# A new issue order for a block-sparse attention and FFN kernel, with thirteen zero matmuls ahead of the first key turn

## The chip, the cores and the metric

The kernel runs on one core of a Trainium2 chip. The metric is the device time of one execution in microseconds, the median of the runs shown. A core has five engines with a queue each: TensorE (PE in the profile, its weight loads PEld), VectorE (DVE), ScalarE (ACT), GpSimd (POOL) and SyncE (SP), which here only issues transfers. Each engine takes the instructions of its queue in order and waits at the head for what the instruction needs.

## The reference

Block-sparse causal attention over 4 batches, 8 heads, 768 positions of width 64, then an FFN on the joined heads. All inputs are float32.

```python
k_rep = k.reshape(B, H, 12, 64, 64).mean(axis=3)            # one mean per block of 64 keys
gate = einsum('bhsd,bhnd->bhsn', q, k_rep)                  # causal blocks only
mask = top 3 blocks of gate, and the row's own block, and key <= query
attn = softmax(where(mask, q @ k.T / 8, -1e9))
x = (attn @ v), heads side by side                          # 3072 x 512
h = x @ w_in                                                # 512 x 2048
out = gelu_tanh(h) @ w_out                                  # 2048 x 512
```

## The kernel before

The work is cut into 16 pairs of heads, p = 0 to 15, four for each batch (b = p // 4). A pair goes through these steps; the line numbers are those of the kernel before, and in the kernel after every one is one higher, since its table of the order is one line longer.

- Loads, issued on SP's queue (L386, L392; the first k and q at L420, k on SP and q on ScalarE's queue). For batch 0 they go to free parts of large tiles, for later batches to a few buffers (`ksd`, `qsd`, `vsd`), which come free when the values have been transposed or cast.
- Turning k and q. In batch 0, TensorE turns them in halves of three tiles (`turn`, L537 for k of pairs 0 and 1, with two more columns that give the sums of the blocks, and L540), and VectorE or ScalarE copies the halves out (L355 is a copy on ScalarE, L357 on GpSimd, L359 on VectorE). Later, VectorE transposes them (`tr`, L556), sums the keys' blocks (`ks`, L613; L575 in batch 0) and spreads the sums (`ksb`, L630).
- The gate (L679): q against the block sums. VectorE finds the third largest per row with MAX8 (L711) and writes a mask (`madd`, L716); TensorE turns the mask (L748), and a copy puts it below q in `qT` (L355 or L359), so that one matmul gives the masked scores.
- Scores (`heads2`, L855 in batch 0; `heads`, L1038 later), the exponential on ScalarE (L874, L1051), the causal triangle by a select on GpSimd (L900, L1065), the products with v (L923, L1077), the division on VectorE (L941, L960), and the result's transposition (`turn_out`, L980).

When a batch's four pairs are through, its FFN follows: `s1` (L1114, matmuls with w_in; L1203 for part of the last batch), GELU on ScalarE (L1126), then the product with w_out. For batch 0 that is plain (L1314). For the others it is Strassen's scheme in seven products per pair of 128-token rows (`half`, L1364), with sums of the inputs on VectorE (L1301), and joins of the products into `osb`, also on VectorE (L1413), stored by SP (L1339, L1448, L1457). Work of the FFN of one batch is interleaved with the scores of the next: it is the filler that TensorE works on while ScalarE makes exponentials. ScalarE has to load another table when it goes from exponentials to GELU and back.

The weights w_in and w_out, 2 MB each in the types of the kernel, are loaded by GpSimd's queue in two parts each (`load_w`, L452). w_in is issued after the last v of batch 0 has come in. The first loads of batch 1 are held back on SP's queue until w_in is there (`hold`, L1559).

Zero matmuls (`warm`, L1516) work on a zeroed tile into a free PSUM bank and have no reader.

Nothing is scheduled at run time or by the compiler. The program builds some 1,900 operations with their dependences, and then issues them in the order of a table; a second table says which buffer an operation takes, in the order in which buffers are asked for, and a third which copies go to ScalarE or GpSimd instead of their first choice (mostly VectorE):

```python
engine = {n: e for e, ops in ENGINE.items() for n in ops}
picks = iter(BUFFER)
for n in ORDER:
    op = self.ops[n]
    for kind, key in op.takes:
        if key not in self.buf:
            self.buf[key] = self.kinds[kind][0][next(picks)]
    op.emit(engine.get(n, next(iter(op.engines))))
```

So `ORDER` sets the order within each engine's queue, and the semaphores follow from the dependences. The four PSUM banks (`bank`) serve turns, gates, masks, products with v and the FFN's second product; two double banks (`wide`) serve scores and the FFN's first product.

Of the kernel before, what the change touches and what calls it, by code (L numbers as in the profile page):

```python
# [21 lines left out]
    6, 0, 1, 1890, 1891, 2, 1892, 1893, 1894, 3, 9, 1895, 1896, 1897, 1898,  # L22
    62, 71, 4, 15, 1899, 1900, 1901, 195, 73, 72, 1902, 64, 12, 75, 18, 22,
    5, 63, 1903, 76, 74, 77, 23, 66, 1904, 1905, 84, 85, 68, 19, 78, 89,
    1906, 26, 1907, 82, 200, 31, 67, 194, 79, 35, 90, 32, 80, 91, 98, 86,
    83, 36, 87, 100, 93, 196, 214, 99, 101, 201, 95, 205, 94, 39, 215, 102,
    197, 1908, 103, 1909, 104, 113, 206, 109, 1910, 115, 114, 1911, 219,
    210, 120, 111, 220, 1912, 118, 121, 105, 40, 106, 1913, 27, 30, 119,
    211, 198, 1914, 1915, 107, 110, 216, 122, 249, 123, 234, 202, 44, 203,
    207, 250, 208, 212, 240, 124, 221, 43, 48, 45, 217, 235, 133, 125, 229,  # L30
    224, 1916, 49, 241, 52, 222, 135, 126, 236, 140, 245, 251, 127, 53, 230,
    268, 225, 138, 57, 56, 141, 246, 129, 1917, 231, 134, 58, 263, 232, 131,
    242, 151, 1918, 238, 130, 155, 237, 243, 157, 139, 142, 269, 254, 143,
    264, 247, 252, 255, 283, 258, 144, 284, 226, 279, 274, 1919, 270, 146,
    227, 280, 256, 1920, 1921, 265, 266, 1922, 147, 145, 271, 275, 292, 276,
    288, 297, 272, 289, 302, 298, 277, 303, 281, 149, 285, 308, 309, 299,
    286, 259, 153, 290, 317, 61, 1923, 300, 293, 260, 304, 305, 318, 169,
    326, 313, 322, 294, 328, 261, 310, 295, 323, 306, 319, 363, 314, 364,
    311, 365, 163, 329, 315, 356, 358, 170, 366, 171, 359, 360, 361, 320,
    324, 327, 367, 362, 352, 353, 354, 355, 357, 330, 408, 409, 410, 411,  # L40
    331, 412, 373, 374, 335, 375, 376, 377, 174, 403, 336, 404, 405, 406,
    388, 407, 389, 175, 178, 390, 391, 393, 394, 395, 396, 392, 418, 397,
    419, 420, 179, 421, 368, 369, 182, 370, 433, 422, 434, 398, 399, 371,
    435, 400, 372, 436, 401, 437, 383, 438, 183, 439, 186, 338, 187, 440,
    402, 441, 384, 378, 385, 386, 339, 442, 443, 387, 444, 379, 380, 445,
    446, 337, 341, 381, 428, 334, 429, 190, 346, 345, 447, 191, 631, 448,
    382, 430, 423, 451, 424, 431, 452, 342, 453, 425, 432, 426, 454, 413,
    414, 632, 455, 427, 343, 344, 415, 449, 416, 456, 417, 457, 347, 458,
    584, 635, 459, 349, 460, 585, 461, 553, 588, 462, 463, 566, 348, 590,
    464, 587, 465, 466, 470, 586, 570, 595, 471, 567, 571, 639, 472, 591,  # L50
    473, 592, 636, 593, 574, 568, 474, 450, 575, 640, 561, 475, 476, 477,
    478, 583, 479, 480, 552, 562, 576, 481, 467, 554, 644, 596, 572, 692,
    645, 557, 598, 482, 483, 650, 484, 648, 485, 569, 558, 488, 622, 489,
    490, 696, 654, 491, 597, 492, 555, 486, 594, 651, 493, 573, 614, 652,
    494, 577, 623, 601, 653, 556, 578, 559, 693, 647, 560, 615, 495, 618,
    496, 563, 497, 564, 616, 498, 602, 603, 705, 605, 646, 706, 499, 619,
    656, 658, 617, 655, 500, 624, 606, 501, 609, 502, 700, 697, 503, 657,
    711, 507, 620, 708, 709, 508, 678, 621, 565, 610, 611, 607, 504, 643,
    661, 625, 715, 679, 509, 712, 626, 662, 665, 701, 713, 957, 666, 510,
    579, 674, 604, 511, 716, 512, 958, 680, 663, 608, 682, 513, 514, 714,  # L60
    612, 515, 613, 516, 675, 717, 468, 517, 718, 683, 580, 669, 961, 518,
    719, 676, 677, 707, 726, 965, 519, 664, 670, 667, 684, 520, 681, 727,
    505, 735, 736, 671, 962, 970, 668, 972, 728, 1020, 521, 722, 522, 971,
    525, 672, 723, 730, 976, 737, 685, 673, 743, 704, 523, 526, 738, 686,
    966, 527, 1024, 974, 1021, 528, 724, 627, 744, 1025, 529, 745, 1033,
    530, 731, 531, 725, 628, 732, 1034, 739, 740, 532, 729, 1037, 981, 733,
    758, 687, 533, 534, 830, 1028, 734, 1039, 741, 535, 742, 746, 756, 536,
    977, 747, 1040, 1044, 537, 748, 538, 978, 1082, 1924, 539, 831, 832,
    979, 1041, 749, 833, 759, 760, 761, 834, 540, 1083, 973, 768, 769, 770,
    762, 1042, 1086, 524, 1043, 548, 1095, 771, 1096, 544, 545, 752, 753,  # L70
    487, 754, 755, 772, 1029, 763, 764, 765, 757, 766, 840, 1087, 841, 1099,
    842, 843, 767, 782, 1036, 783, 784, 785, 844, 786, 792, 549, 793, 969,
    794, 795, 773, 1032, 835, 796, 836, 837, 982, 838, 825, 826, 546, 1035,
    1101, 774, 541, 1090, 1144, 827, 839, 828, 984, 811, 775, 829, 1145,
    812, 985, 1157, 813, 814, 1148, 1158, 815, 1161, 845, 787, 1152, 788,
    789, 1149, 1105, 1153, 790, 1163, 846, 1045, 806, 542, 807, 808, 809,
    1102, 1164, 1410, 847, 791, 801, 802, 810, 803, 1411, 980, 804, 777,
    1165, 778, 805, 1159, 779, 780, 816, 781, 817, 818, 1103, 819, 849, 850,
    1002, 1166, 1104, 797, 820, 1156, 1418, 851, 1107, 852, 821, 853, 1048,
    854, 822, 989, 988, 855, 856, 798, 859, 823, 990, 860, 1098, 857, 861,  # L80
    862, 863, 858, 799, 1091, 997, 1003, 864, 865, 547, 866, 1419, 998,
    1414, 550, 991, 551, 992, 993, 868, 1473, 1474, 994, 869, 1004, 1010,
    1047, 1011, 870, 1094, 867, 776, 871, 999, 1012, 1006, 800, 995, 1005,
    872, 1068, 873, 1007, 874, 1169, 1069, 1064, 824, 1008, 996, 1000, 875,
    1055, 1009, 877, 1065, 1072, 878, 848, 876, 1056, 1073, 879, 1051, 1109,
    1110, 1013, 1477, 880, 1059, 1066, 1478, 1052, 885, 886, 887, 1097,
    1001, 1053, 888, 1117, 1060, 1014, 1070, 889, 1067, 1061, 1106, 890,
    891, 1118, 892, 882, 881, 895, 1423, 1481, 896, 1160, 1134, 883, 1071,
    1486, 893, 897, 1119, 894, 1126, 1074, 898, 899, 900, 1167, 901, 902,
    1135, 903, 1054, 1425, 1130, 904, 1539, 1075, 1172, 905, 1127, 906,  # L90
    1121, 1131, 1136, 1057, 1132, 1424, 1535, 1058, 907, 908, 1168, 1540,
    1426, 909, 1113, 1114, 1062, 910, 1128, 1076, 911, 913, 914, 915, 1122,
    1171, 1115, 1536, 1063, 1129, 1123, 1188, 1116, 1189, 1133, 1196, 1015,
    1120, 1487, 1137, 916, 1197, 1124, 1198, 1190, 912, 1179, 917, 921,
    1077, 1192, 1125, 922, 923, 1490, 1180, 1193, 924, 1183, 925, 926, 927,
    928, 1548, 931, 932, 1181, 1488, 1194, 1184, 1138, 1415, 1139, 1185,
    1175, 933, 934, 1191, 1195, 1235, 1199, 1176, 1177, 935, 1209, 929, 936,
    1178, 1236, 937, 1422, 1543, 938, 930, 1492, 940, 1549, 1182, 1186, 941,
    1200, 942, 1211, 1212, 1597, 1482, 943, 944, 1187, 1552, 1201, 1427,
    945, 946, 1213, 1237, 947, 1202, 1496, 1238, 1598, 1489, 939, 1601,  # L100
    1429, 949, 1214, 1554, 950, 1215, 1493, 1555, 948, 1430, 1264, 1265,
    951, 1494, 1266, 1267, 1239, 1230, 1231, 1495, 1268, 1232, 1233, 1269,
    1270, 1602, 1271, 1558, 1272, 1556, 1234, 1273, 1544, 1216, 1217, 952,
    1218, 1610, 1219, 1205, 1220, 1206, 1550, 1207, 1431, 1432, 1208, 1559,
    1611, 1254, 1551, 1434, 1614, 1210, 1255, 1256, 1257, 1240, 953, 1258,
    1241, 1547, 1242, 1243, 1245, 1246, 1616, 1247, 1244, 1248, 1259, 1260,
    1261, 1497, 1262, 1249, 1221, 1485, 1222, 1223, 1263, 1433, 1557, 1224,
    1498, 919, 1288, 1289, 1225, 1290, 1501, 1617, 1291, 1250, 1283, 1284,
    1620, 918, 1292, 1285, 1286, 1287, 1251, 1500, 1278, 1274, 1279, 1280,
    1281, 1435, 1293, 1294, 1438, 1295, 1621, 1560, 1296, 1613, 1302, 1226,  # L110
    1303, 1282, 1618, 1227, 1304, 1297, 1305, 1455, 1228, 1517, 1306, 1442,
    1619, 1437, 1518, 1307, 1275, 1298, 1252, 1308, 1309, 1312, 1313, 1519,
# [1506 lines left out]
```

## Time and profile before

| | us |
|---|---|
| median of 3 runs | 257.85 (257.77 to 258.06) |
| profiled execution | 257.31 |
| its span | 255.4 |
| TensorE busy | 246.1 (96%) |
| VectorE busy | 191.2 (75%) |
| ScalarE busy | 174.8 (68%) |
| GpSimd busy | 87.6 (34%) |
| bytes moved | 32.61 MB, mean 128 GB/s |

The span is the time from the first to the last instruction that the profiler records; the execution's own time is 1.9 us longer. An engine's busy time counts its instructions and leaves out waits. TensorE's busy time flatters it, since its matmuls are pipelined and overlap: a matmul of 384 columns has a duration of 326 ns on the page, while 54 of them in a row take 8.78 us, 163 ns each.

### The profile page before, as it was taken

Reading aid. Unit: us, or ns where it says so; the run is one execution under the profiler, and the core shown is the slowest. Engines: PE = TensorE matmul, PEld = TensorE weight load, DVE = VectorE, ACT = ScalarE, POOL = GpSimd, SP = SyncE. Lnnn points to the kernel's source line nnn. Section 1 sums busy time; section 2 is a strip of 40 time slices with the busy share of each in tenths; the row PEclk is TensorE's granted clock in tenths of the full one; section 3 lists DMA queues with packets and bytes.
Section 4 is the critical chain, followed back from the end, with each engine's and each line's share of the span. In section 5 each row is a group of like instructions: output and inputs, shape, how many; then the busy total and the mean of one; then the engine's idle time right before and its main releaser. Section 6 shows DMA issues by size and latency. Waiting matters only on the chain.

```text
span 255.4 us, 6432 instructions
## 1 busy us (share of the span) xinstructions
PE 246.1 (96%) x2485; PEld 171.8 (67%) x2485; DVE 191.2 (75%) x537; ACT 174.8 (68%) x222; POOL 87.6 (34%) x168
## 2 busy tenths in 40 slices
PE   6999999999999899899999999999999999999994
PEld 5676676655556465565678888665778887666883
DVE  2588853016887997998999888999977675777953
ACT  2469887643888899667798885566999865557300
POOL 8637753002255465212175655030155410000000
PEclk9999999999999999999999999999999999999999
DMA  8998699999999899999497896930511421020024
GB/s 162 219 205 170 98 213 135 191 172 158 158 167 151 171 192 140 216 138 183 83 163 161 156 120 124 153 108 13 131 59 39 107 74 42 3 82 0 3 82 164
DMA packets 130926, 32.61 MB, mean 128 GB/s; under 512 B 124528, under 2 KB 126928, under 8 KB 130896
## 3 DMA queue, kind: packets, MB, share of 16 engines
q1 hardware_dynamic: 126160, 27.62, 61.9%
q0 software_dynamic: 3136, 4.19, 10.2%
q10 hardware_dynamic: 1600, 0.39, 0.7%
q8 instruction: 19, 0.31, 0.5%
q14 instruction: 11, 0.09, 0.1%
HBM read 27.26 MB, written 6.29 MB: 131 GB/s over the span
## 4 chain that ended last, share of the span: by engine, by line
PE 81%; DVE 6%; DMA 3%; POOL 3%; ACT 2%; SPq 1%; issue 1%; DVEq 0%; POOLq 0%; ACTq 0%
PE wide L1114 26%; PE bank L1364 22%; PE wide L1038 8%; PE wide L1203 5%; PE bank L1077 5%; PE bank L1314 4%; DMA sd<-in_k_dram 3%; PE wide L855 3%; PE bank L679 2%; PE bank L923 2%; DVE s L556 2%; SPq L392 1%; DVE ks L613 1%; PE bank L980 1%; PE bank L540 1%
## 5 line engine op out<-in xcount | busy, mean ns | idle before, releaser
L1114 PE MATMUL wide<-xT,w_in 128*128 128x384 f16 x416 | 73.8, 326 | 0.0
L1051 ACT ACTIVATE ats<-wide 128x896 f16<-128x896 f32 x72 | 62.6, 916 | 7.1 <-PE wide L1038 3.7
L1126 ACT ACTIVATE G<-wide 128x768 f16<-128x768 f32 x52 | 42.0, 810 | 27.5 <-PE wide L1114 25.4
L1114 PEld LDWEIGHTS <-w_in 128*128 128x128 f16 x416 | 39.8, 98 | 26.1 <-issue 0.8
L1065 POOL TENSOR_SCALAR_AFFINE_SELECT ats<-ats 128x256 f16<-128x256 f16 x72 | 32.4, 462 | 56.4 <-ACT ats L1051 55.9
L1038 PE MATMUL wide<-qT,kT 76*128 76x512 f16 (+3 forms) x192 | 38.9, 305 | 0.1
L556 DVE STREAM_TRANSPOSE s<-sd 128x768 f32<-128x768 f32 x24 | 23.1, 968 | 16.9 <-DMA sd<-in_k_dram 15.0
L1364 PE MATMUL bank<-w_out,G 128*128 128x256 f16 x216 | 33.4, 272 | 0.0
L1314 PE MATMUL bank<-w_out,G 128*128 128x512 f16 x96 | 29.7, 379 | 1.2 <-ACT qT L355 1.2
L1364 PEld LDWEIGHTS <-G 128*128 128x128 f16 x288 | 26.8, 98 | 5.4
L357 POOL CAST kT<-s 64x768 f16<-64x768 f32 x22 | 18.7, 854 | 29.5 <-DVE s L556 28.8
L1077 PEld LDWEIGHTS <-ats 128*128 128x128 f16 x504 | 23.0, 97 | 5.0 <-POOL v L357 0.3
L1077 PE MATMUL bank<-v,ats 128*128 128x65 f16 x504 | 25.5, 194 | 0.0
L1413 DVE TENSOR_TENSOR osb<-bank,osb 128x512 f32<-128x512 f32 (+1 forms) x38 | 22.0, 592 | 3.2 <-PE bank L1364 2.9
L1038 PEld LDWEIGHTS <-kT 76*128 76x128 f16 x192 | 17.1, 98 | 9.4 <-issue 0.6
L874 ACT ACTIVATE ats<-wide 128x1024 f16<-128x1024 f32 (+3 forms) x24 | 21.0, 919 | 3.3 <-PE wide L855 3.1
L1364 PEld LDWEIGHTS <-XS 128*128 128x128 f16 x216 | 20.1, 97 | 4.2
L1364 PE MATMUL bank<-TS,XS 128*128 128x256 f16 x144 | 22.4, 272 | 0.0
L357 POOL CAST v<-vsd 128x768 f16<-128x768 f32 x13 | 11.7, 908 | 19.0 <-DMA vsd<-in_v_dram 18.9
L961 DVE TENSOR_TENSOR xn<-bank,zr 128x384 f16<-128x384 f32 x24 | 13.4, 557 | 0.8
L1314 PEld LDWEIGHTS <-G 128*128 128x128 f16 x96 | 8.9, 97 | 7.5 <-issue 2.5
L711 DVE MAX8 sel<-sel 128x8 f32<-128x12 f32 x160 | 13.3, 157 | 0.6
(119 smaller groups left out, 360.9 us busy)
## 6 DMA issues: line engine op xcount, KB each, us to landing
out_dram<-osb SPq DMA_DIRECT2D x23, 256.0 KB
vsd<-in_v_dram SPq DMA_DIRECT2D x26, 192.0 KB
sd<-in_k_dram SPq DMA_DIRECT2D x48, 96.0 KB
sd<-in_q_dram SPq DMA_DIRECT2D x48, 96.0 KB
w_in<-in_moe_w_in_dram POOLq DMA_DIRECT2D x2, 1024.0 KB, 10.8
w_out<-in_moe_w_out_dram POOLq DMA_DIRECT2D x2, 1024.0 KB, 12.8
G<-in_k_dram SPq DMA_DIRECT2D x4, 192.0 KB
G<-in_q_dram SPq DMA_DIRECT2D x4, 192.0 KB
```

The costliest lines, as they stand in the source:

```text
L357: nc.gpsimd.tensor_copy(out=out, in_=in_)
L556: nc.vector.transpose(out=T[key + "T32", p], in_=T[key, p].rearrange("p t j -> p (t j)"))
L874: nc.scalar.activation(out=T["at", u][:, :, 0:n], in_=plan.buf[("st",) + u].rearrange("p (h w) -> p h w", h=2)[:, :, 0:n], func=AF.Exp, bi ...
L1038: nc.tensor.matmul(st[:, x:e], kT16[i][h][0:76, s0:s0 + 128], qT16[i][h][0:76, s0 + (x - cb):s0 + (e - cb)], start=True, stop=True)
L1051: nc.scalar.activation(out=T["at", u][:, 0:n], in_=plan.buf[("st",) + u][:, 0:n], func=AF.Exp, bias=0.0, scale=SCALE)
L1065: nc.gpsimd.affine_select(out=dg, in_=dg, compare_op=ALU.is_ge, fill=0.0, base=0, pattern=[[0, 2], [1, 128]], channel_multiplier=-1)
L1077: nc.tensor.matmul(pvv[:, qc, 0:65], at[:, cb + (qc - jc) * 128: cb + (qc - jc + 1) * 128], v16[i][:, jc, h, :], start=(gi == 0 and jc == ...
L1114: nc.tensor.matmul(hps[:, 512 * e:512 * e + HALF], w_in16[:, ci, (2 * j + e) * 128: (2 * j + e + 1) * 128], T["xT", b][:, ci, HALF * h:HAL ...
L1126: nc.scalar.activation(out=G[:, :, h, j, :], in_=plan.buf["hps", b, j, h].rearrange("p (e w) -> p e w", e=2)[:, :, 0:HALF], func=AF.Gelu_a ...
L1314: nc.tensor.matmul(plan.buf["ops", b, ti], G[:, f % 2, 2 * ti // NC, f // 2, ti % (NC // 2) * 128:ti % (NC // 2) * 128 + 128], w_out16[:, ...
L1364: nc.tensor.matmul(dst[:, HD * h:HD * h + HD], FACT[m][0][:, j, t * 128:(t + 1) * 128], FACT[m][1][:, j, :], start=(clear and j == 0), sto ...
L1413: nc.vector.tensor_tensor(out=dst(), in0=src(), in1=other(), op=ALU.add)
```

## The change

Only the three tables change: `ORDER`, `BUFFER` and `ENGINE`. The operations are the same, but for one zero matmul fewer (38 for 39). Of `ORDER`, which has 1,668 numbers before and 1,667 after, here are the first rows, the rows with the issue of w_out (operation 163), and the last:

```diff
 ORDER = [
-    6, 0, 1, 1890, 1891, 2, 1892, 1893, 1894, 3, 9, 1895, 1896, 1897, 1898,
-    62, 71, 4, 15, 1899, 1900, 1901, 195, 73, 72, 1902, 64, 12, 75, 18, 22,
-    5, 63, 1903, 76, 74, 77, 23, 66, 1904, 1905, 84, 85, 68, 19, 78, 89,
-    1906, 26, 1907, 82, 200, 31, 67, 194, 79, 35, 90, 32, 80, 91, 98, 86,
...
-    242, 151, 1918, 238, 130, 155, 237, 243, 157, 139, 142, 269, 254, 143,
...
-    311, 365, 163, 329, 315, 356, 358, 170, 366, 171, 359, 360, 361, 320,
...
+    4, 2, 0, 1890, 1891, 1892, 1893, 1894, 1895, 1896, 6, 1897, 15, 1898, 9,
+    1899, 1900, 1901, 12, 1, 1902, 62, 18, 71, 64, 195, 1903, 73, 72, 63,
+    75, 82, 1904, 22, 1905, 1906, 23, 76, 66, 1907, 31, 19, 74, 35, 77, 36,
+    84, 98, 68, 85, 3, 99, 5, 83, 78, 194, 44, 200, 79, 80, 100, 89, 67,
...
+    129, 126, 127, 241, 138, 231, 245, 242, 254, 139, 153, 255, 157, 1918,
+    131, 246, 140, 232, 268, 269, 238, 237, 141, 270, 142, 130, 163, 258,
...
+    1841, 1868, 1864, 1867, 1847, 1865, 1866, 1869, 1870, 1872, 1871, 1880,
+    1878, 1877, 1874, 1873, 1879, 1876, 1883, 1881, 1884, 1886, 1885, 1843,
+    1882, 1887, 1888, 1844, 1842, 1846, 1927, 1848]
...
 ENGINE = {
     "ACT": [
-        67, 72, 74, 85, 90, 110, 114, 119, 121, 139, 141, 331, 348, 449,
-        467, 486, 504, 523, 541, 580, 594, 597, 628, 657, 716, 749, 857,
-        893, 980, 981, 1043, 1044, 1105, 1167, 1168, 1202, 1496, 1620, 1621,
-        1655, 1674, 1677, 1698, 1704, 1707, 1727, 1736, 1786, 1822],
+        67, 72, 74, 90, 99, 101, 110, 114, 119, 121, 139, 331, 345, 346,
+        348, 449, 467, 486, 504, 523, 541, 580, 598, 628, 654, 657, 716,
+        749, 857, 893, 929, 980, 981, 1043, 1044, 1105, 1106, 1167, 1168,
+        1202, 1346, 1497, 1558, 1620, 1668, 1674, 1677, 1698, 1707, 1727,
+        1736, 1786, 1822],
     "POOL": [
...
-        1159, 1160, 1425, 1426, 1488, 1489, 1550, 1551, 1613]}
+        337, 586, 587, 646, 647, 707, 708, 972, 973, 1035, 1036, 1097, 1159,
+        1160, 1425, 1426, 1488, 1489, 1551, 1613]}
```

Numbers from 1890 on are the zeros; 6 and 12 are the first loads of k, 9 and 15 of q; 0 to 5 are constants; 62 and 66 turn pair 0's k, 71 and 73 its q; 75 and 78 are its gates, 194 and 200 its first scores; 89 and 93 turn pair 1's k; 157 and 163 issue w_in and w_out; 1842 to 1844 are in the seventh product of a pair of token rows of batch 3, 1846 its join and 1848 its store. In words, by engine:

- TensorE: thirteen zeros stand ahead of the first turn of keys (62), nine before. The first scores (194) stand right behind pair 0's second gate (78); the turns of pair 1's keys (89, 93), the first of which lay between, come later. Scores of pairs 4 to 7 stand closer together, with fewer of batch 0's FFN matmuls between them. The kernel's last matmuls (1844, 1842) belong to product seven of the second pair of token rows in batch 3; before they belonged to product two of the third pair.
- SP: v of pair 0 is loaded as two consecutive halves; k and q of pair 6 and the first part of k of pair 7 go ahead of v of pair 5; batch 0's results are stored later among the loads; k of pair 11 comes before that of pair 10.
- ScalarE's queue: the second half of pair 0's q is issued ahead of its first.
- GpSimd: two memsets of constants (ones) come first; w_out (163) is issued one select behind w_in (157), where ten operations lay between before.
- Engines of copies: eight go from ScalarE to VectorE, twelve the other way, two casts from GpSimd to VectorE.

More of the change, by code (lines that the diff above doesn't have):

```diff
@@ L21 @@
 ORDER = [
[128 rows of a table removed]
-BUFFER = [
[23 rows of a table removed]
[128 rows of a table added]
+BUFFER = [
[23 rows of a table added]
 ENGINE = {
     "ACT": [
[4 rows of a table removed]
[5 rows of a table added]
     "POOL": [
-        337, 586, 587, 646, 647, 707, 708, 972, 973, 1035, 1036, 1097, 1098,
-        1159, 1160, 1425, 1426, 1488, 1489, 1550, 1551, 1613]}
+        337, 586, 587, 646, 647, 707, 708, 972, 973, 1035, 1036, 1097, 1159,
+        1160, 1425, 1426, 1488, 1489, 1551, 1613]}
 class Op:
```

287 rows, old and new, of tables (BUFFER, ORDER) are left out of this document.

## The prediction

> **What bounds the kernel now.** I read the page first, then the windows by stage, then TensorE's waits, the chain of waits, and last the timelines around each place where TensorE stood still. The page of the kernel before:
>
> ```profile
> span 255.4 us, 6432 instructions
> PE 246.1 (96%) x2485; PEld 171.8 (67%) x2485; DVE 191.2 (75%) x537; ACT 174.8 (68%) x222; POOL 87.6 (34%) x168
> L556 DVE STREAM_TRANSPOSE s<-sd 128x768 f32<-128x768 f32 x24 | 23.1, 968 | 16.9 <-DMA sd<-in_k_dram 15.0
> ```
>
> TensorE is busy for 96% of the span, so a new order can gain only where TensorE stands still or goes slowly. The windows (us, then busy us of PE, PEld, DVE, ACT, POOL, then clock, DMA share, GB/s) say where:
>
> ```profile
> 0.00:10.00 10.00, 7.54 (x42) 5.59 (x43) 2.94 (x28) 2.44 (x4) 8.69 (x31) 1.00 1.01 183
> 10.00:20.00 10.00, 8.98 (x118) 6.96 (x119) 8.34 (x38) 6.59 (x12) 3.90 (x10) 1.00 1.20 213
> 60.00:80.00 20.00, 19.89 (x162) 10.46 (x160) 15.98 (x58) 15.61 (x21) 7.44 (x12) 1.00 1.03 156
> 80.00:90.00 10.00, 8.83 (x99) 5.35 (x98) 8.64 (x27) 8.14 (x11) 5.59 (x11) 1.00 0.92 178
> 90.00:100.00 10.00, 10.00 (x128) 6.51 (x127) 7.93 (x16) 9.28 (x13) 5.98 (x13) 1.00 1.15 153
> 100.00:110.00 10.00, 8.99 (x80) 5.18 (x78) 9.59 (x38) 7.42 (x10) 4.55 (x6) 1.00 1.29 186
> 110.00:180.00 70.00, 70.00 (x669) 49.24 (x667) 64.57 (x169) 51.22 (x66) 24.64 (x40) 1.00 0.77 128
> 180.00:252.00 72.00, 71.98 (x702) 55.81 (x699) 53.99 (x110) 44.89 (x54) 12.17 (x25) 1.00 0.20 62
> ```
>
> From 110 to 252 us TensorE is busy for 141.98 of 142 us: nothing is to be had there. Missing are 2.46 us before 10, 1.02 from 10 to 20, 1.17 in 80 to 90 and 1.01 in 100 to 110. The start holds more than that, because busy matmuls there overlap work that waits: its pace is set by the exponentials on ScalarE. Here are TensorE's and ScalarE's timelines (start, us, line, shape, count, idle before and its releaser):
>
> ```profile
> 1.07 2.10 PE L1516 MATMUL bank<-XS 128*128 128x256 f16 x9 [1.07 <-DVE bmask L284]
> 4.18 1.64 PE L537 MATMUL bank<-identk,G 128*128 128x130 f32 x6 [1.01 <-DMA G<-in_k_dram]
> ...
> 8.44 0.96 PE L537 MATMUL bank<-identk,G 128*128 128x130 f32 x6
> ...
> 10.22 0.37 PE L679 MATMUL bank<-s,ksbx 128*32 128x96 f32 x8
> 10.52 0.94 PE L537 MATMUL bank<-identk,G 128*128 128x130 f32 x6
> ...
> 11.61 0.28 PE L855 MATMUL wide<-XS,XS 64*128 64x256 f16 x2
> ...
> 10.32 0.37 ACT L355 COPY XS<-bank 128x256 f16<-128x256 f16 x1 [2.07 <-DVE XS L359]
> ...
> 12.35 1.51 ACT L874 ACTIVATE ats<-wide 128x1024 f16<-128x1024 f32 x2 [0.38 <-PE wide L855]
> 14.52 1.94 ACT L874 ACTIVATE ats<-wide 128x1024 f16<-128x1024 f32 x2 [0.66 <-PE wide L855]
> 18.09 0.48 ACT L355 CAST XS<-bank 128x384 f16<-128x384 f32 x1 [1.64 <-DVE ks L575]
> ...
> 38.61 1.30 ACT L874 ACTIVATE ats<-wide 128x256 f16<-128x256 f32 x2 [0.52 <-PE wide L855]
> ```
>
> The first score is at 11.61, the first exponential at 12.35, the last ends at 39.91, and the FFN of batch 0 can't begin in earnest before. Two stalls remain; the chain of waits gives both (start, us, what):
>
> ```profile
> 77.35 4.16 DMA sd<-in_k_dram
> 81.59 0.99 DVE s L556
> 82.60 0.95 DVE ks L613
> 83.59 0.50 DVE qT L359
> 84.11 0.69 ACT qT L355
> 84.84 0.59 PE bank L1314 x2
> ...
> 93.83 4.68 DMA sd<-in_k_dram
> 98.63 0.99 DVE s L556
> ...
> 101.85 0.98 DVE s L556
> 102.87 0.48 PE bank L679 x8
> ```
>
> In the first, k of pair 7 lands late, VectorE stands before its transpose (L556), and the mask copies of pair 6 (qT, on VectorE and ScalarE), which need nothing of pair 7, are queued behind it. In the second, k and q of pair 9 are late themselves, and pair 9's gate (L679) waits. TensorE's idle times there are those missing in the windows, 1.17 and 1.01. Both go back to the loads, and the loads to the weights:
>
> ```profile
> 26.72 1.66 POOL L452 DMA_DIRECT2D w_in<-in_moe_w_in_dram  x2
> ...
> 38.52 1.78 POOL L452 DMA_DIRECT2D w_out<-in_moe_w_out_dram  x2
> ...
> 41.11 9.76 SPq L392 DMA_DIRECT2D sd<-in_k_dram  x4
> ...
> 63.44 1.25 SPq L386 DMA_DIRECT2D vsd<-in_v_dram  x2
> ...
> 70.65 0.82 POOL L357 CAST v<-vsd 128x768 f16<-128x768 f32 x1
> ```
>
> The four issues of pair 4's k need 9.76 us on SP's queue, from 41.11, while w_out moves. Just ahead of that the transfers run thin, at 73 GB/s, because w_in is in and w_out was issued late:
>
> ```profile
> 40.00:42.00 2.00, 2.00 (x26) 1.35 (x23) 0.00 (x0) 1.94 (x3) 0.30 (x1) 1.00 0.83 73
> ```
>
> **The change, part by part.** Instructions keep their shapes; what changes is their order on each queue, buffers, and the engine of some twenty copies. By the two engine tables ScalarE gets four operations more, VectorE two fewer, GpSimd two fewer.
>
> Zeros. Thirteen instead of nine stand ahead of the first turn: 13 x 2.10/9 = 3.03 us from 1.07, to 4.10, so the first turn still waits for k at 4.18. Cost: nothing, the cover being the 1.01 us of idle time; without it four zeros, 0.93. All told there is one zero fewer: -0.1 at about half that price, since the clock is open later.
>
> Start. The first score is placed right behind the gate, ahead of the six turns of 10.52, so it moves from 11.61 to about 10.52 (-1.09). The mask's copy at 10.32 goes from ScalarE to VectorE; q's second half is issued ahead of its first on ScalarE's queue, GpSimd's memsets ahead of other work: these feed the same gate, and I put them at nothing, with 0.37 (that copy) as their price. Of ScalarE's later waits the 1.64 us before 18.09 is for a sum of keys that now stands earlier. Walking after's order with durations of this trace, the exponentials end about 2.7 us earlier. I take -2.2, because q of pair 3 and v of pair 1 are now loaded later. Bounds: -0.7 (1.09 less 0.37: no later wait goes) and -3.2 (1.09, 1.64 and the 0.52 before 38.61).
>
> Weights and loads. w_in follows the same number of selects on GpSimd, so it comes as much earlier as the exponentials before it, about 2 us. w_out is issued one select behind w_in, instead of 11.8 us later, so the thin stretch at 40 us closes, another 1.5 us by its length in the trace. The stream of q, k and v behind it starts some 3.5 us earlier. In it the v of pair 5 is moved behind k6, q6 and part of k7, and the first stores of results behind loads: ahead of k7 lie 0.54 MB less, ahead of q9 1.15 MB less. At the 156 GB/s of 60 to 80 us this is 3.5 and 7.4 us. So k7 lands 7.0 earlier, q9 10.9.
>
> Both stalls. TensorE reaches these places earlier too: 2.2 from the start, and the order packs the scores of pairs 4 to 7 into 24.5 us of matmuls (28.2 before; each matmul by its start-to-start time in the trace), which is 3.7. That is 5.9 against k7's 7.0, and about 7.1 against q9's 10.9 with the first stall gone. Both stalls go: -1.17 - 1.01 = -2.2. The mask copies of pair 6 also no longer stand behind k7's transpose. The margin at k7 is only 1.1 us.
>
> The packed stage. ScalarE has 23.3 us of work in those 24.5, 95%, counted in the same way from its queue in after's order. The row of 90 to 100 us, with ScalarE at 93% and TensorE losing nothing, gives 0; the other end is that its two waits come back, about 2.0. I take +0.7, nearer to that row. The four extra copies on ScalarE lie in this figure or behind 110 us, where it is busy 51.22 of 70. Two casts go from GpSimd to VectorE (about 0.5 each, as qT's copy at 83.59): VectorE has 5.4 us free between 110 and 180, which hides them; without that cover 1.0.
>
> End. After's last matmuls are product seven of a pair of token rows of batch 3, whose join is 512 wide; before's are product two, with a join of 256. Two rows of VectorE's joins:
>
> ```profile
> 242.71 0.68 DVE L1413 TENSOR_TENSOR osb<-bank,osb 128x512 f32<-128x512 f32 x1
> ...
> 252.08 0.42 DVE L1413 TENSOR_TENSOR osb<-bank,osb 128x256 f32<-128x256 f32 x1 [0.18 <-PE bank L1364]
> ```
>
> That is +0.26 for the join, and a store of 256 KB instead of 128, for which I add 0.1 (0 to 0.25): +0.35.
>
> Sum: -2.2 - 2.2 - 0.1 + 0.7 + 0.35 = -3.45. The profiled execution took 257.31 us, its span 255.4 and 1.9 around it; it should come to 253.9. The median of the runs, 257.85, is 0.54 above the profiled one: **254.4**. Its own ends are 257.85 - 3.2 - 2.2 - 0.1 + 0.3 = 252.6 and 257.85 - 0.7 - 2.2 - 0.1 + 2.0 + 0.5 = 257.4.
>
> **The rivals.**
>
> The clock opens earlier. Six turns take 1.64 us at 4.18 and 0.96 at 8.44, so the slow clock lasts until about 8 in this trace. With TensorE busy from 1.07 on without the idle 1.01 us, it might open sooner: six turns of q at 0.11 less each are 0.7, so 253.7. Against it: the turns then wait for q's loads instead. The Trainium skill ("TensorE: Matmul & The Clock Gate", Part 1) says that the clock opens after about one busy window of 3.4 us, and that the window runs free of the kernel's start. By that rule it would open between some 4.5 and 8 us in after; the trace of before, with its gap and its slow turns up to 8, agrees with it but does not test it.
>
> The stalls come back as waits for ScalarE, at 95% in the packed stage. Then only start and end count: 257.85 - 2.2 - 0.1 + 0.35 = 255.9. For it speaks that every stage here runs near one engine's limit; against it the row of 90 to 100.
>
> The start gives nothing, since q3, v1 or a copy on VectorE (8.34 of 10 us busy between 10 and 20) is late instead: 257.85 - 2.2 - 0.1 + 0.7 + 0.35 = 256.6, with up to 2.0 for the packed stage 257.9.
>
> Slower: the loads bound the middle. VectorE already waits 15.0 us in all for k. If w_out ends no earlier than before, k7 comes 3.5 earlier by its place alone, against 3.7 of matmuls that no longer lie ahead of it: the gains of the start and of the first stall turn into waits for k, and 0.2 more. The v of pair 5, issued from 63.44 on and cast at 70.65, is moved behind what takes up to 7.4 us; from the end of its issues at 64.69 to the cast are 5.96, so it is 1.4 late for products that TensorE takes in order. The second stall goes all the same (7.4 by place): 257.85 + 0.2 + 1.4 - 1.0 + 0.35 - 0.1 = 258.7. Each us that the weights end earlier comes off this, so it decides where they gain less than 0.3. The Trainium skill ("DMA: Bandwidth & Descriptors", the section on queues, rings and completion order) says that an engine takes turns between its queues packet by packet. By that rule w_out issued early would slow the loads beside it rather than go ahead of them; the 9.76 us of k4's issues agree, but in after the first of those loads still waits for w_in's last part, so the total of bytes decides, and I leave the chance low.
>
> **How the numbers follow.** Forecast 0.53, clock 0.05, ScalarE's waits 0.14, no gain at the start 0.13, loads 0.15. The range goes from 252.0 (the forecast's low end less the clock) to 257.9 (the top of the third rival), which leaves out the last rival and a few hundredths below. A measurement of this kernel tells about 0.2% from no change, 0.5 us. Faster than 257.3: the first three and most of the fourth, less the forecast's upper end, 0.74. Within 257.3 to 258.4: 0.08. Slower: the loads, and mishaps at the packed stage, 0.18.
>
> **What would show it.** Right: the first score near 10.5 and the last exponential's end near 37.5; GpSimd's issue of w_out within 3 us of w_in's; no wait of TensorE at L1315 or L680 of a microsecond; the last join 0.68. Wrong: TensorE idle for k or v in 55 to 85 us, waits of L1039 or L1078 on ScalarE there, or a later end of the first exponentials.

## The result, and the profile after

The kernel after takes 254.02 us, the median of four runs (253.93 to 254.13), beside 257.81 us for the kernel before (257.68 to 258.06): a ratio of 0.985, 95% interval 0.9835 to 0.9869. The forecast was 254.4. Its profiled execution took 253.93 us, where 253.9 was worked out. The sum came out, but the experiments below show that two of its mechanisms were not the ones that I had named.

Later sets of runs were made on other occasions, and there the kernel before spread from 255.7 to 259.2; each experiment is therefore compared with the runs of before in its own set, by its ratio and interval. The first number given is always the median.

The page of the kernel after, and its windows (columns as in the prediction):

```profile
span 252.2 us, 6437 instructions
PE 244.2 (97%) x2484; PEld 170.2 (67%) x2484; DVE 188.8 (75%) x535; ACT 177.5 (70%) x226; POOL 84.0 (33%) x166
```

```profile
0.00:10.00 10.00, 6.71 (x47) 4.56 (x48) 3.39 (x28) 2.40 (x4) 8.62 (x31) 1.00 1.01 181
...
60.00:80.00 20.00, 20.00 (x168) 10.61 (x167) 15.60 (x57) 17.86 (x24) 7.06 (x12) 1.00 1.21 150
80.00:90.00 10.00, 9.53 (x124) 6.03 (x121) 9.60 (x29) 9.14 (x12) 7.14 (x13) 1.00 0.96 153
90.00:100.00 10.00, 10.00 (x139) 6.28 (x136) 9.38 (x19) 9.83 (x13) 5.53 (x12) 1.00 0.77 150
100.00:110.00 10.00, 10.00 (x63) 5.85 (x61) 9.69 (x35) 7.85 (x10) 2.80 (x4) 1.00 1.12 143
```

TensorE now misses 0.47 us between 80 and 90 and nothing between 100 and 110, against 1.17 and 1.01: 1.71 us regained. From 90 to 100 ScalarE is busy for 9.83 of 10 us and TensorE still loses nothing. The start, TensorE and then ScalarE:

```profile
1.07 2.95 PE L1517 MATMUL bank<-XS 128*128 128x256 f16 x13 [1.07 <-DVE bmask L285]
4.39 0.91 PE L538 MATMUL bank<-identk,G 128*128 128x130 f32 x6 [0.37 <-DMA G<-in_k_dram]
6.77 0.52 PE L541 MATMUL bank<-identk,G 128*128 128x128 f32 x3 [1.47 <-DMA G<-in_q_dram]
7.12 0.27 PE L1517 MATMUL bank<-XS 128*128 128x256 f16 x1
7.23 0.49 PE L541 MATMUL bank<-identk,G 128*128 128x128 f32 x3
...
10.40 0.37 PE L680 MATMUL bank<-s,ksbx 128*32 128x96 f32 x8
10.71 0.28 PE L856 MATMUL wide<-XS,XS 64*128 64x256 f16 x2
...
36.21 1.94 ACT L875 ACTIVATE ats<-wide 128x1024 f16<-128x1024 f32 x2 [0.41 <-PE wide L856]
```

The first score is at 10.71 (11.61 before; 10.5 was expected), and the last exponential ends at 38.15 (39.91; 37.5 was expected), so the start gives 1.76. The six turns at 4.39 take 0.91 us instead of 1.64: TensorE is at its full pace right behind the zeros, where before it came to it only at about 8.4. The clock column of the windows shows 1.00 there in both kernels; only the pace of the matmuls tells the two apart. The first half of q, now issued second, is waited for until 6.77 (1.47 us), and this eats much of what the early pace won: the second gate is at 10.40, later than the 10.22 of before. What moved the first score is its place right behind that gate.

The weights and the loads behind them (GpSimd, then SP's queue):

```profile
25.83 0.20 POOL L451 COPY after_in<-vsd 1x16 f32<-1x16 f32 x1 [0.79 <-DMA vsd<-in_v_dram]
26.36 1.66 POOL L453 DMA_DIRECT2D w_in<-in_moe_w_in_dram  x2 [0.34 <-issue]
...
28.66 1.78 POOL L453 DMA_DIRECT2D w_out<-in_moe_w_out_dram  x2
...
41.08 0.58 SPq L1560 DMA_DIRECT2D after_in<-w_in  x1
41.70 7.58 SPq L393 DMA_DIRECT2D sd<-in_k_dram  x4
```

In before the hold on w_in (`after_in`) was released earlier:

```profile
40.49 0.58 SPq L1559 DMA_DIRECT2D after_in<-w_in  x1
```

w_in is issued 0.36 us earlier than before, not 2: GpSimd waits there for the last v of batch 0, which SP issues from 20.06 on, 0.54 later than in before. w_out does follow directly. But w_in releases SP's hold 0.59 later than in before (from its issue to there are 14.7 us, 13.8 in before, and 13.8 to 14.8 in the other runs, with w_out early or late), so the loads of batch 1 start no earlier. Pair 4's k has all its issues out at 49.28 (50.87 before), because they take 7.58 us instead of 9.76: the loads gained 1.6 us at this place and not 3.5. What brings that is w_out's place. In the runs below these four issues take 7.0 to 8.1 us where w_out is early, and 9.6 to 10.8 where it is not. What is left of the first stall, and the end (TensorE, VectorE, SP):

```profile
85.25 0.48 PE L680 MATMUL bank<-s,ksb 128*32 128x160 f32 x8 [0.47 <-DVE ksb L631]
...
248.12 0.27 PE L1517 MATMUL bank<-XS 128*128 128x256 f16 x1
...
248.32 0.69 DVE L1414 TENSOR_TENSOR osb<-bank,osb 128x512 f32<-128x512 f32 x1 [0.23 <-PE bank L1365]
...
249.07 0.33 SPq L1449 DMA_DIRECT2D out_dram<-osb  x1
```

Pair 7's gate waits 0.47 us for its key sums, which VectorE, busy for 9.60 of 10 us in that window, comes to late. The last join is 512 wide, as expected. From the last matmul's end at 248.39 to the span's end are 3.8 us.

### The profile page after: what moved, and what is told of

It is laid out like the page before. It is cut to its first block, busy times and chain, and to the rows that moved or that the text cites. A ratio compares the mean times of both kernels' runs of the same rounds, so it can differ in the third digit from the quotient of the medians.

```text
span 252.2 us, 6437 instructions
## 1 busy us (share of the span) xinstructions
PE 244.2 (97%) x2484; PEld 170.2 (67%) x2484; DVE 188.8 (75%) x535; ACT 177.5 (70%) x226; POOL 84.0 (33%) x166
## 4 chain that ended last, share of the span: by engine, by line
PE 80%; SPq 8%; DMA 4%; DVE 3%; POOL 2%; issue 1%; DVEq 0%; POOLq 0%
PE wide L1115 27%; PE bank L1365 22%; PE wide L1039 9%; SPq L387 7%; PE bank L1315 6%; PE wide L1204 6%; PE bank L1078 5%; DMA vsd<-in_v_dram 2%; PE bank L680 2%; SPq L393 2%; DMA sd<-in_k_dram 1%; DMA G<-in_q_dram 1%; PE bank L924 1%; PE wide L856 1%; PE bank L981 1%
## 5 line engine op out<-in xcount | busy, mean ns | idle before, releaser
L1115 PE MATMUL wide<-xT,w_in 128*128 128x384 f16 x416 | 74.8, 326 | 0.0
L1066 POOL TENSOR_SCALAR_AFFINE_SELECT ats<-ats 128x256 f16<-128x256 f16 x72 | 31.0, 443 | 51.1 <-ACT ats L1052 37.5
L1365 PE MATMUL bank<-w_out,G 128*128 128x256 f16 x216 | 32.6, 272 | 0.0
L1365 PEld LDWEIGHTS <-G 128*128 128x128 f16 x288 | 26.9, 98 | 5.5
L1315 PE MATMUL bank<-w_out,G 128*128 128x512 f16 x96 | 28.8, 379 | 0.0
L358 POOL CAST kT<-s 64x768 f16<-64x768 f32 x20 | 16.9, 855 | 33.0 <-DVE s L557 32.4
L1078 PE MATMUL bank<-v,ats 128*128 128x65 f16 x504 | 24.9, 194 | 0.0
L358 POOL CAST v<-vsd 128x768 f16<-128x768 f32 x13 | 11.1, 858 | 22.9 <-DMA vsd<-in_v_dram 15.7
L356 ACT CAST qT<-s 64x768 f16<-64x768 f32 x15 | 12.4, 830 | 0.3
```

Source lines behind the costliest of these rows:

```text
L358: nc.gpsimd.tensor_copy(out=out, in_=in_)
L1066: nc.gpsimd.affine_select(out=dg, in_=dg, compare_op=ALU.is_ge, fill=0.0, base=0, pattern=[[0, 2], [1, 128]], channel_multiplier=-1)
L1078: nc.tensor.matmul(pvv[:, qc, 0:65], at[:, cb + (qc - jc) * 128: cb + (qc - jc + 1) * 128], v16[i][:, jc, h, :], start=(gi == 0 and jc == ...
L1115: nc.tensor.matmul(hps[:, 512 * e:512 * e + HALF], w_in16[:, ci, (2 * j + e) * 128: (2 * j + e + 1) * 128], T["xT", b][:, ci, HALF * h:HAL ...
L1315: nc.tensor.matmul(plan.buf["ops", b, ti], G[:, f % 2, 2 * ti // NC, f // 2, ti % (NC // 2) * 128:ti % (NC // 2) * 128 + 128], w_out16[:, ...
L1365: nc.tensor.matmul(dst[:, HD * h:HD * h + HD], FACT[m][0][:, j, t * 128:(t + 1) * 128], FACT[m][1][:, j, :], start=(clear and j == 0), sto ...
```

## The experiments

Operations have the numbers of the change's section. A run's line numbers are those of before, plus one or two, by the length of its table.

**The start alone on the kernel before (b_start).** All 253 operations of batch 0's attention take after's order, buffers and engines in the slots that they have in before.

```diff
 # ORDER of before: the positions of batch 0's operations keep, what stands in them changes
-6, 0, 1, 1890, 1891, 2, 1892, ... (before's order of the 253)
+4, 2, 0, 1890, 1891, 1892, 1893, ... (after's order of the same 253)
```

> The kernel before with all operations of batch 0's attention (loads, zeros, turns, gates, scores, exponentials, products with v) in after's order, buffers and engines; the weights' issues, all loads of later batches and everything behind stay as before. Theory 1 (the start's lead of 1.85 us runs into loads that come only some 1.5 us earlier, because w_out's issue follows the last select): stalls at 84.8 and 102.9 stay and grow by a few tenths, about 256.3. Rival, the start is independent of the loads: 255.9. Rival, loads bound the middle: both stalls grow by all that the start gained, 257.8.

It took 256.61 us (254.77 to 257.72), ratio 0.9971 (0.9946 to 0.9996). That is 0.8 less than before in this set (257.38), where the first theory had 1.5 less and the third none. TensorE's waits in its profiled execution (line, releaser, us in all, times, longest), which took 257.6:

```profile
PE bank L1315 <- ACT qT L356: 1.2, 1, 1.2
...
PE bank L680 <- DVE s L557: 1.0, 1, 1.0
PE bank L680 <- DVE ksb L631: 0.8, 1, 0.8
```

Both stalls are there, with a third beside them. In this execution the last exponential ends at 39.01, 0.90 earlier than in before, but between 80 and 90 us TensorE misses 1.93 us, 0.76 more than in before. The start's lead is mostly taken back in the middle: whoever arrives earlier waits longer.

The same start also ran differently. Here are the zeros, the first turns of k and the next, from this run:

```profile
1.07 2.95 PE L1517 MATMUL bank<-XS 128*128 128x256 f16 x13 [1.07 <-DVE bmask L285]
4.48 1.64 PE L538 MATMUL bank<-identk,G 128*128 128x130 f32 x6 [0.46 <-DMA G<-in_k_dram]
...
9.45 1.30 PE L538 MATMUL bank<-identk,G 128*128 128x130 f32 x6
```

After the same thirteen zeros the turns are slow, and even those at 9.45 are mostly so. When full pace comes is thus not fixed by the program. The Trainium skill ("TensorE: Matmul & The Clock Gate", Part 1) says that the clock opens after a busy window of about 3.4 us and that the window runs free of the kernel's start. That the same instructions come to full pace at 4.4 us in the one trace and at about 10 in the other agrees with a window that runs free. But 10 is 9 us after the first zero, more than two such windows (6.8 us, an estimate from the Trainium skill's figure); whether the waits between kept a window from counting as busy, no run here shows.

**w_out early, alone (b_wout).** One operation of before moves on GpSimd's queue.

```diff
-157, 270, 265, 145, 276, 285, 299, 61, 304, 310, 319, 163
+157, 270, 163, 265, 145, 276, 285, 299, 61, 304, 310, 319
```

> The kernel before with one operation moved: the issue of w_out on GpSimd stands one select behind that of w_in, nothing else. Theory 1 (the early w_out is what brought the loads forward, by about 2 us, and that is enough): both stalls go, 257.8 - 2.2 = 255.6. Rival (the places of k7 and q9 among the loads matter as much): one stall stays in part, 256.3 to 256.9. Rival (w_out beside w_in slows it, and the start of the FFN waits): 258 or more.

It took 257.01 us (256.29 to 257.9), ratio 0.9998 (0.9975 to 1.0022): no gain clear of the noise, and my theory fell. In its profile the first stall is gone but for 0.2 us, and the second stands at full size, as TensorE's waits show:

```profile
PE bank L680 <- DVE s L557: 1.0, 1, 1.0
...
PE bank L1315 <- ACT qT L356: 0.2, 1, 0.2
```

The timelines say why: SP's queue first, then GpSimd's.

```profile
83.60 0.38 SPq L393 DMA_DIRECT2D sd<-in_q_dram  x1
87.76 0.38 SPq L387 DMA_DIRECT2D vsd<-in_v_dram  x1
```

```profile
85.82 0.77 POOL L1066 TENSOR_SCALAR_AFFINE_SELECT ats<-ats 128x256 f16<-128x256 f16 x2 [1.55 <-ACT ats L1052]
86.55 1.19 POOL L358 CAST v<-vsd 128x768 f16<-128x768 f32 x1
```

SP's queue stands from 83.98 to 87.76. Next in it is the load of pair 8's v, which needs one of the two `vsd` buffers, and that comes free when GpSimd has cast pair 6's v, at 87.74; the cast is queued behind selects that wait for ScalarE. Behind v8 stand k9 and q9. In the kernel before it is the same, only that SP comes there later and waits less:

```profile
86.06 0.38 SPq L392 DMA_DIRECT2D sd<-in_q_dram  x1
87.44 0.39 SPq L386 DMA_DIRECT2D vsd<-in_v_dram  x1
```

So the time of the cast, not the number of bytes, set when k9 and q9 were loaded, and 2 us of earlier transfers were spent on waiting longer at this place. That accounts for the second stall; the first stall's 1 us was won. In the profiled execution it is taken up at the start, where the last exponential ends at 40.87, 0.96 later than in before; whether w_out's place delays it is not shown (40.50 in b_wout_v8, whose start is the same, and 39.90 in b_wout_v8_13). After's table has v8 far behind q9.

**w_out early, and v8 behind q9 (b_wout_v8).**

```diff
 # on top of b_wout, SP's queue
-958, 468, 961, 965, 505, 962, 1020, 966, 1024, 1021, 1025
+958, 468, 961, 505, 962, 1020, 1024, 1021, 1025, 965, 966
```

> The kernel before with two moves: the issue of w_out one select behind w_in (as in b_wout, which gave no gain), and the two issues of pair 8's v on SP's queue behind those of pair 9's q. Theory 2, new: the second stall is not a matter of bytes; SP's queue stands at the load of pair 8's v until GpSimd has cast pair 6's v (1.0 us in before, from 86.44 to 87.44; 3.8 in b_wout, where the queue came there 2 us earlier), and k9 and q9 are queued behind. Then both stalls go, about 2.0 less than before: 255.4 beside a before of 257.4. Rival (bytes: pair 8's v is only 0.4 MB, 2.5 us at 156 GB/s): the second stall goes in part, 256.3. Rival (the loads have no part in it): no change, 257.4.

It took 255.69 us (255.21 to 256.39), ratio 0.9936 (0.9914 to 0.9957): 1.9 less than before (1.6 by the ratio), where 2.0 was expected. Of the two stalls, its waits show only what is left of the first:

```profile
PE bank L1315 <- ACT qT L356: 0.2, 1, 0.2
```

**These two moves and after's start (b_three).** The order is that of b_start and b_wout_v8 together.

> The kernel before with the two moves of b_wout_v8 and batch 0's attention in after's order. Theory 2 (the start's lead is kept only when no load stops it; in b_start the second stall took it all): start and stalls add up, 257.4 - 2.0 - 1.5 = 253.9, as fast as after. Rival (the closer packing of pairs 4 to 7 and the places of the other loads are needed too): the first stall stays, 255 or more.

It took 253.99 us (253.69 to 254.24), ratio 0.9867 (0.9836 to 0.9899). That is after's time, with everything behind batch 0 in before's order but for the two moves. The closer packing of pairs 4 to 7, the other reordered loads and the engines of the later copies were not needed for it.

**Without w_out's move (b_v8_13, and b_wout_v8_13 beside it).** Here v8 stands behind q9 and four zeros stand ahead of the first turn, in before's order otherwise; beside it the same with w_out's move.

```diff
 # zeros, both kernels
-1898, 62, 71, 4, 15, 1899, 1900, 1901, 195, 73, 72, 1902
+1898, 1899, 1900, 1901, 1902, 62, 71, 4, 15, 195, 73, 72
```

> As b_wout_v8_13 without the move of w_out. Theory 3 (w_out's early issue brings k7 forward by about 2 us, and only that takes the first stall away): the first stall stays and takes up what the zeros won, 254.0 + 1.2 to 254.0 + 2.5, 255.2 to 256.5. Rival (the second stall's queue was all that mattered): 254.0.

> The kernel before with three moves and nothing else: w_out's issue one select behind w_in, pair 8's v behind pair 9's q on SP's queue (b_wout_v8, 255.69), and four zeros put ahead of the first turn of keys, where they stand behind it. Theory 3 (the start's gain is the clock, and the zeros make it: after with nine zeros took 255.69, as much as b_wout_v8 with nine): 254.0, the whole of the change by three moves. Rival (the reordered start counts by itself): 255 to 255.7.

They took 255.87 us (255.13 to 257.34; ratio 0.9945, 0.992 to 0.997) and 255.68 us (255.17 to 256.25; ratio 0.9931, 0.9914 to 0.9949). The profile without w_out's move has the first stall again, 1.3 us at L1315, in a run of 257.34; but the times of the two don't differ beyond their intervals. So v8's place is shown to matter, and w_out's is seen in the waits but not settled in the time.

The second of the two also broke my third theory, that the zeros alone are the start's gain. Full pace comes at about 7 us here, later than in after and earlier than in before, and TensorE's timeline shows what takes the gain:

```profile
4.38 1.64 PE L538 MATMUL bank<-identk,G 128*128 128x130 f32 x6 [0.35 <-DMA G<-in_k_dram]
...
7.55 0.83 PE L538 MATMUL bank<-identk,G 128*128 128x130 f32 x6
...
9.39 0.37 PE L680 MATMUL bank<-s,ksbx 128*32 128x96 f32 x8
10.30 0.91 PE L538 MATMUL bank<-identk,G 128*128 128x130 f32 x6 [0.54 <-DMA G<-in_k_dram]
...
11.36 0.28 PE L856 MATMUL wide<-XS,XS 64*128 64x256 f16 x2
```

The second gate is at 9.39, 0.8 earlier than in before, as the four zeros also stand in its way no longer. Then pair 1's k stands ahead of the first scores in before's order, and it isn't loaded until 10.30. The first score gains 0.25.

**Nine zeros, with the new order.** Twice: in the kernel after (a_nine), and in b_three (b_three_nine).

```diff
 # after
-1899, 1900, 1901, 12, 1, 1902, 62, 18, 71, 64
+12, 1, 62, 18, 71, 1899, 1900, 1901, 1902, 64
```

> The kernel after with four of the thirteen zeros behind the first turns instead of ahead of them. Theory 1 (the four zeros keep TensorE busy, the clock opens at about 4.4 us instead of 8; the early clock shortens the turns, but q's load hides most of it): six turns of k take 1.64 again, the first score is 0.3 later, 254.3. Rival (the clock's opening is not due to the zeros): turns at 0.9 as in after, 254.0. Rival (the clock is worth all of the slow turns): 255.

> b_three (253.99) with four of its thirteen zeros behind the first turns. Theory 4 (the early clock and the reordered start are worth something only together: zeros without the order gave 255.68, and neither gave 255.69; with the order but a late clock, the gate itself comes late): 255.7. Rival (the order alone is worth most of it, and after with nine zeros was slow for another reason): 254.3 or less.

After with nine zeros took 255.69 us (255.42 to 256.25; ratio 0.9939, 0.9919 to 0.9959), 1.7 more than after in the first set of runs; none of my figures was that high. b_three with nine took 255.06 us (254.75 to 255.75; ratio 0.991, 0.9893 to 0.9926), 1.1 more than with thirteen, between the two theories. TensorE in after with nine zeros:

```profile
1.07 2.10 PE L1518 MATMUL bank<-XS 128*128 128x256 f16 x9 [1.07 <-DVE bmask L286]
4.48 1.64 PE L539 MATMUL bank<-identk,G 128*128 128x130 f32 x6 [1.31 <-POOL cgate L475]
6.78 0.88 PE L542 MATMUL bank<-identk,G 128*128 128x128 f32 x3 [0.66 <-DMA G<-in_q_dram]
7.44 1.27 PE L1518 MATMUL bank<-XS 128*128 128x256 f16 x5
8.51 0.85 PE L542 MATMUL bank<-identk,G 128*128 128x128 f32 x3
...
10.28 1.51 PE L539 MATMUL bank<-identk,G 128*128 128x130 f32 x6
```

The turns at 10.28 are still slow. With the gap of 1.3 us behind the zeros and that ahead of q, full pace comes only at about 11.7. But the slow pace is not all that these two runs change. The first turn of q starts at 6.78, as in after (6.77), so the slow turns of k up to there cost nothing. Behind it the four moved zeros stand in the path: five zeros take from 7.44 to 8.51, where after has one from 7.12 to 7.23. That is 0.96 of the 1.95 us by which the first score comes later, at 12.66, and part of this is slow pace too; the slow pace of the other matmuls makes up the other half. A run with the four zeros left out would separate the two, and there is none.

With the stalls out of the way, the four cases of the start stand side by side: before's order with nine zeros 255.69 and with thirteen 255.68; after's order with nine 255.06 and with thirteen 253.99. To have the four zeros in the idle time and not behind the first turns is worth 1.1 us there (the runs lie apart, the intervals of the two ratios just overlap) and 1.7 in after, both with the new order, and nothing with the old. The order with nine zeros gained 0.6, within the overlap of the intervals.

What the start gains is then kept whole. In all ten profiled executions in which neither stall stands at its size, with either order and either place of the zeros, 215.5 to 215.8 us lie between the end of the last exponential and the end of the execution; in before it is 217.4.

**q's halves in the old order, and the gap closed.** In a_q0 the first half of q is issued first again; a_q0z also puts three zeros into the wait for the second half.

```diff
 # a_q0
-15, 1898, 9
+9, 15, 1898
 # a_q0z, also
-1903, 73, 72, 63, 75, 82, 1904, 22, 1905, 1906
+1903, 1904, 1905, 1906, 73, 72, 63, 75, 82, 22
```

> The kernel after with the first half of pair 0's q issued ahead of the second on ScalarE's queue, as before. In after TensorE waits 1.47 us for it at 6.77. Theory 1 (gate, mask and first score hang on it): the first half is turned near 5.6, the gate follows the turn of the second half at about 7.2 instead of 7.85, the first score comes about 0.6 earlier, and the end too: 253.4. Rival (the exponentials or k's second half set the pace): no change, 254.0.

> The kernel after with the first half of pair 0's q issued first (a_q0) and three zeros moved ahead of the turn of q's second half, into the 0.77 us in which TensorE waits there. Theory 3 (after's rare late runs, 255.3 and 255.9, are runs in which the waits for q keep the clock from opening; with the gaps closed it opens in nearly every run): 253.6, no run above 254.5. Rival (late runs come from something else): 253.9 with one run in three or four late.

They took 253.95 us (253.58 to 254.06; ratio 0.9873, 0.9843 to 0.9903) and 253.79 us (253.51 to 254.09; ratio 0.986, 0.9841 to 0.9878). The first score came to 10.21 and 10.12, 0.5 and 0.6 earlier than in after, as expected, but at the end only 0.1 to 0.3 of it is left, within the intervals. The rest goes among the exponentials, the last of which end at 38.31 and 37.94 (38.15 in after). In a_q0 TensorE waits there for GpSimd's cast of a v:

```profile
18.86 0.66 PE L925 MATMUL bank<-v,ats 128*128 128x65 f16 x12 [0.99 <-POOL v L359]
```

None of the ten runs of these two took more than 254.1 us. Of after's own ten runs two took over 255, and of a_tail's six, which have after's start, three over 254.9. That fits the theory that the wait for q can cost the pace, but ten runs don't settle it.

**The end, and after again.** In a_tail the second pair of token rows is finished ahead of the third, as in before.

```diff
-1871, 1880, 1878, 1877, 1874, 1873, 1879, ..., 1885, 1843, 1882, 1887, 1888, 1844, 1842, 1846, 1927, 1848
+1871, 1843, 1844, 1842, 1880, 1878, 1846, 1877, 1848, 1874, 1873, 1879, ..., 1885, 1882, 1887, 1888, 1927
```

> The kernel after with the second pair of token rows of batch 3 finished ahead of the third, as before: product seven, its join and its store stand ahead of the last products. Theory (after's last store of 256 KB behind a join of 512 ends the kernel 4.1 us after the last matmul, before's 3.5): 0.5 less than after, 253.5. Rival (the last transfer's fixed part decides): as after, 254.0.

> The kernel after unchanged, beside the others on one chip. Theory (runs of before spread over 3.5 us here because the clock opens at another moment in each run, and after, with thirteen zeros, spreads less): 254.0, within 1 us of each other. Rival (the spread is a matter of the chip): after spreads as widely as before.

a_tail took 254.47 us (253.72 to 256.02; ratio 0.9896, 0.9857 to 0.9934), after 254.07 (253.56 to 255.92; ratio 0.9891, 0.9852 to 0.9931). No gain; in the profiled execution 3.86 us lie behind the last matmul's end, 3.8 in after. (The expectation's 4.1 and 3.5 us count from that matmul's start.) VectorE's last row in a_tail shows that its joins now queue:

```profile
246.62 2.48 DVE L1415 TENSOR_TENSOR osb<-bank,osb 128x512 f32<-128x512 f32 x5 [1.60 <-PE bank L1366]
```

They end at 249.10, and after's at 249.01. Of after's six runs four lie between 253.56 and 254.09, and two at 255.28 and 255.92, so it does not always keep within 1 us. A late or falling clock would explain the two, but neither was profiled; the mean granted clock was 0.993 in the first and 1.000 in the second, and 0.993 is also that of b_three's profiled execution, in which the clock fell for a while (last section) and which took 254.15.

## Why the prediction was right, and where it was not

- **The start: -2.2 forecast, -1.76 by the last exponential.** The size is about right; the cause was half seen. I put the four zeros at nothing and the clock's opening in a rival at 0.05 with a price of 0.7. The runs show that the zeros' place carries 1.1 to 1.7 us, and only with the new order of the start. In a_nine about half of it is the zeros' own time in the path, and the other half the slow pace of the matmuls around them. I had counted the zeros only where they arrive, in idle time, and not that before has nine of them between the first turn and the first score, and after five. The rival's price left out the gate, the later turns and the other matmuls, up to 11.7 in a_nine, which are slow as well when full pace comes late.
- **Weights and loads: the step that failed.** w_in's 2 us were 0.36, since GpSimd waits for the last v, where in before its selects kept it longer; and w_in came in 0.59 later, not earlier. What the loads gained came from k4's issues, which take 2.2 us less with w_out issued early. And "ahead of q9 1.15 MB less ... 7.4 us" had the wrong mechanism: SP's queue stood at v8 for a buffer. b_wout has the second stall at full size although its transfers are earlier, and b_wout_v8 shows that v8's place takes it away. I had listed v8's queue among bytes and not looked at what its first instruction waits for, though the gap of 1.0 us between 86.44 and 87.44 stands in SP's timeline of before.
- **Both stalls: -2.2 forecast, -1.71 by the windows.** They went, but for 0.47 at pair 7's gate. It is left on VectorE's queue, not for want of data: VectorE waits for no load in after from 74 to 90.
- **The packed stage: +0.7 forecast, nothing measured.** ScalarE at 9.83 of 10 us cost TensorE nothing, and from 60 to 80, with ScalarE at 17.86 of 20, TensorE missed nothing either. The row that I leaned on (9.28) was the right one; the allowance on top of it was the error.
- **The end: +0.35 forecast.** Before's last matmul is in this row:

```profile
251.88 0.27 PE L1516 MATMUL bank<-XS 128*128 128x256 f16 x1
```

  From its end at 252.15 to the span's end were 3.25 us, now 3.8: +0.56. But a_tail shows that the old order of the end would not bring it back in this kernel.
- **The sum.** The parts of the profiled executions are -1.76, -1.71, 0 and +0.56; with -0.29 elsewhere between the last exponential and the last matmul, and -0.18 outside the span, they make -3.38, where -3.45 was forecast. Two gains over-stated by 0.93 stand against 0.7 charged for nothing, so that the total came out so closely is in part luck.
- **The rivals.** The loads' rival, that an earlier start turns into waits, is what b_start does. It did not decide in the kernel after, where w_out comes early and v8 is out of the way.

## What to carry to other kernels

When a transfer comes late, look first at what its queue's head is waiting for: an issue that waits for a buffer holds back all loads behind it, and an earlier start upstream only lengthens that wait. A stall near the middle can take back a gain ahead of it, as with the start in b_start, and a late load can take back an early gate, as with the zeros in the old order. So edits that bring little alone can be worth their price together; test them together as well as one by one. And when an instruction is moved into idle time, count what it no longer delays at its old place.

## What the runs showed of the hardware

The same thirteen zeros led to turns of 0.91 us in one execution and of 1.64 in another. In b_three the first six turns were fast, and those after TensorE's wait of 1.65 us for q were slow again:

```profile
4.43 0.91 PE L538 MATMUL bank<-identk,G 128*128 128x130 f32 x6 [0.44 <-DMA G<-in_k_dram]
6.99 0.65 PE L541 MATMUL bank<-identk,G 128*128 128x128 f32 x3 [1.65 <-DMA G<-in_q_dram]
...
9.42 1.44 PE L538 MATMUL bank<-identk,G 128*128 128x130 f32 x6
```

The clock column (the third number from the end) of this run's windows shows the fall:

```profile
6.00:8.00 2.00, 1.01 (x6) 0.97 (x7) 0.09 (x1) 0.32 (x1) 1.86 (x3) 0.81 1.37 220
8.00:10.00 2.00, 2.00 (x17) 1.32 (x16) 1.63 (x8) 0.64 (x2) 1.83 (x8) 0.50 1.35 216
10.00:12.00 2.00, 2.00 (x33) 1.62 (x33) 1.34 (x6) 0.55 (x2) 0.69 (x3) 0.83 1.31 214
```

So after a pause of under 2 us the granted clock can fall to half, here for some 3.4 us by these windows. The slow turns at the start of before, b_start and a_nine stand in windows with 1.00: there the column doesn't show the slow pace, and only the matmuls' durations do.

More zeros ahead of the first turn make early full pace likely and not certain. In the five profiled executions with nine, TensorE comes to it at 8.4 us or later; in eight of the nine with thirteen it comes by 7.2, b_three then loses it, and in b_start it comes at about 10.

That b_three took 254.15 us all the same shows that the pace of the very first turns is not what counts. Its full pace is back ahead of the first score, at 11.65. In b_three with nine zeros the second gate, at 12.62, is still slow (0.45 us, 0.37 in after), and the first score comes at 13.00. The last exponentials of the two end at 38.68 and 40.28, 1.60 apart, and so do the executions, 254.15 and 255.75.
